# Pooled attention feeding a mixture of experts: values pooled in their own pair, slot inverse built in the first pair, last mixing in the score banks, expert 2's gathers issued earlier, three double banks for the first layer

## The chip, the cores and the metric

The kernel runs on one core of a Trainium2 chip. The metric is the device time of one execution in microseconds (us). "Clock" is the share of full speed that the throttle granted to TensorE (PE). The other engines are VectorE (DVE), ScalarE (ACT) and GpSimd (POOL); POOL also issues most DMA. A time "in the trace" counts from the span's start; an execution takes about 1.8 us more than its span. A bank is a piece of PSUM, the memory that PE's matmuls write here; DVE or ACT must copy a result out (evacuate it) before its bank is written again. Mixing is the product of attention weights and values. The slot inverse is the table that tells, for each slot of an expert, which row of x it takes. A gather fetches rows of x by index, a scatter writes output rows by index, both by DMA.

## The reference, cut to what matters

```python
# q, k, v: (8, 8, 576, 64).  Keys and values are pooled by 8 along the sequence.
k_p = k.reshape(B, H, 72, 8, D).mean(axis=3);  v_p = v.reshape(B, H, 72, 8, D).mean(axis=3)
attn = softmax(q @ k_p.T / sqrt(D));  x = attn @ v_p          # then (4608, 512): one row per token
for e in range(8):                                            # routing by a given domain_id
    out[domain_id == e] = relu(x[domain_id == e] @ w1[e]) @ w2[e]     # 512 -> 1024 -> 512
```

## The kernel before: the parts that matter

Four pairs of batches pass through attention; 16 score units and 9 mixing units a pair. Each expert has 640 slots, in five blocks of 128. The program is one list per engine, in order, made from a plan of fractional time slots (16 a pair). An instruction that has to wait holds up all that stands behind it on its engine.

```python
def big():   return ps.tile([128, 2, 512], F32, tag="big",   bufs=2)   # 2 double banks: scores, layer one
def wide():  return ps.tile([128, 8, 128], F32, tag="wide",  bufs=1)   # 1 double bank: mixing, transposes
def small(): return ps.tile([128, 512],    F32, tag="small", bufs=2)   # 2 single banks: all else
...
def av_unit(pr, cc):                                  # mixing of one chunk of 128 rows
    pv = wide();  # 8 heads of matmuls into pv
    # DVE: rcp <- 1/pv[..., 64];  x_sb <- pv * rcp;  after each third chunk x_lin <- x_sb by DMA
...
def gather(e, j, rows=XROWS): ...                     # POOL: xg[e % 2][:, j] <- rows of x_lin by index
def turn_units(e, j0, j1):                            # PE transposes xg into "wide", DVE copies to xT
def l1_units(e, ...): p = big();   ...                # 8 units: matmuls, then ReLU by ACT or DVE in turn
def l2_units(e, ...): p = small(); ...                # 1 unit per block: matmuls, copy, scatter to out
...
# the plan (slots): vp_units pool v, kp_units pool k, qt_units transpose q, all ONE PAIR AHEAD
put(kp_units(pr + 1), t0 + k0, t0 + k1); put(vp_units(pr + 1), t0 + k1, t0 + k2); put(qt_units(pr + 1), t0 + k2, t0 + k3)
put([perm_prep], 17.3, 17.3)                          # slot inverse: one set of DVE compares per pair,
for i in range(NP):                                   # then 9 matmuls; sets stand in pairs 1 and 2
    put(perm_units(i), 18.0 + 8 * i, 25.0 + 8 * i); put([perm_mm(i)], 26.5 + 8 * i, 26.5 + 8 * i)
put([perm_finish], 52.0, 52.0); put([orig_finish], 58.0, 58.0); put([count], 61.0, 61.0)
for h in range(12): put([dummy], 48.4 + h, 48.4 + h)  # 12 idle matmuls in pair 3
put([gather(0, j, XE) for j in range(3)], 57.0, 60.0); put([gather(1, j, XE) for j in range(3)], 60.0, 63.0)
put(wload_units(1, 0, 1) + wload_units(1, 1, 1), 63.1, 63.2)          # both weights of expert 1
...
run(l2_units(0, EARLY, CAP, h0))                      # experts 0 and 1 end like this:
for j in range(NBL): gather(2, j)
run(wload_units(3, 0, 1)); run(l2_units(1, EARLY, CAP, h1)); run(wload_units(3, 1, 1))
run(turn_units(2, 0, NBL))
for e in range(2, E): ...                             # l1(e) with gathers of e+1, l2(e) with transposes of e+1
```

The softmax here doesn't subtract the row's maximum and nothing guards it: scores larger than these inputs give would overflow.

## Time and profile before

| reading | value | view |
|---|---|---|
| timed runs | median 277.59 us (276.91 to 278.04) | times |
| span of the first trace | 279.4 us (that execution took 281.21) | page |
| loads | DMA share 1.0 from 10 us on | stage windows |
| first scores of pairs 0 to 3 | 20.4, 42.7, 63.8, 85.9 us | timeline of PE |
| expert 0 starts, expert 2 starts | 106.1, 156.7 us | timeline of PE |

The page shows the span in 40 equal slices; each digit is a busy share in tenths, PEclk the clock in tenths.

```profile
PE   0878878888998659988895799999989999989991
...
PEclk9999999796899956999999599999999999999997
DMA  6999999999997148937973899989979979912022
```

PE is nearly full after the middle; DMA is full until slice 12. The clock falls to 5 in two places. The stage windows give, for each stretch in us, its length, busy us and instructions of PE, PEld, DVE, ACT and POOL, then clock, DMA share and GB/s:

```profile
core 0: us, PE busy (x) PEld busy (x) DVE busy (x) ACT busy (x) POOL busy (x), PEclk, DMA share, GB/s
...
20.00:40.00 20.00, 16.41 (x258) 12.21 (x258) 6.92 (x21) 13.58 (x26) 2.11 (x4) 1.00 1.03 216
...
140.00:160.00 20.00, 14.74 (x81) 7.80 (x80) 4.46 (x8) 2.54 (x6) 11.71 (x12) 0.83 0.63 151
...
200.00:240.00 40.00, 38.37 (x256) 23.05 (x254) 13.55 (x20) 9.12 (x14) 23.87 (x26) 1.00 0.93 195
```

In 20:40 the DVE works 6.92 of 20 us. In 140:160 PE works only 14.74 of 20 us, at clock 0.83. The timelines show why. Columns: start, duration, engine, line, operation, out<-in, shape, count, and in brackets the idle time before with what ended it. First PE, then POOL:

```profile
142.26 7.07 PE L597 MATMUL small<-w,hT 128*128 128x512 f16 x32
151.06 0.40 PE L560 MATMUL turn<-ident,xg 128*128 128x128 f16 x4 [1.73 <-DMA xg<-x_lin,xrow]
...
154.96 0.61 PE L560 MATMUL turn<-ident,xg 128*128 128x128 f16 x4 [0.77 <-DMA xg<-x_lin,xrow]
156.35 0.59 PE L560 MATMUL turn<-ident,xg 128*128 128x128 f16 x4 [0.78 <-DVE xT L561]
```

```profile
146.79 0.98 POOL L606 DMA_INDIRECT out_dram<-y,tok  x1 [0.65 <-ACT y L604]
148.08 1.05 POOL L546 DMA_INDIRECT xg<-x_lin,xrow  x1 [0.30 <-issue]
```

From 149.3 to 156.4 PE does single transposes, each behind its own gather. The gathers start only at 148.08, because they stand on POOL behind the last scatter of expert 0's second layer (146.79). The view by source line puts this much idling before the mixing down to its evacuation (us, times):

```profile
  DVE x_sb L489: 12.4, 18
```

This row adds two engines that overlap: 4.8 us of PE and 7.6 us of its weight loads (PEld), as the page's groups and the view of `x_sb` show. So PE itself idled 4.8 us there.

Lastly, the dense part had pauses of 0.2 to 1.4 us in experts 2 to 6; this is one of the long ones:

```profile
206.07 1.25 PE L581 MATMUL big<-xT,v 128*128 128x320 f16 x8 [1.34 <-issue]
```

### The profile page before, as it was taken

Reading aid. Unit: us, or ns where it says so; the run is one execution under the profiler, and the core shown is the slowest. Engines: PE = TensorE matmul, PEld = TensorE weight load, DVE = VectorE, ACT = ScalarE, POOL = GpSimd, SP = SyncE. Lnnn points to the kernel's source line nnn. Section 1 sums busy time; section 2 is a strip of 40 time slices with the busy share of each in tenths; the row PEclk is TensorE's granted clock in tenths of the full one; section 3 lists DMA queues with packets and bytes.
Section 4 is the critical chain, followed back from the end, with each engine's and each line's share of the span. In section 5 each row is a group of like instructions: output and inputs, shape, how many; then the busy total and the mean of one; then the engine's idle time right before and its main releaser. Section 6 shows DMA issues by size and latency. Waiting matters only on the chain.

```text
span 279.4 us, 5003 instructions
## 1 busy us (share of the span) xinstructions
PE 236.5 (85%) x2060; PEld 148.4 (53%) x2060; DVE 125.0 (45%) x284; ACT 93.0 (33%) x157; POOL 101.1 (36%) x116
## 2 busy tenths in 40 slices
PE   0878878888998659988895799999989999989991
PEld 0666565664674336545552465655645655645640
DVE  7351449687878754432321134333333333243420
ACT  1048475484586623322220130221221311211310
POOL 7001002000000072048417864565646655724042
PEclk9999999796899956999999599999999999999997
DMA  6999999999997148937973899989979979912022
GB/s 111 216 221 212 213 219 237 239 237 245 239 229 181 60 140 161 226 91 135 241 181 123 159 221 263 169 226 189 244 164 174 235 150 196 258 61 114 20 76 106
DMA packets 18153, 50.19 MB, mean 180 GB/s; under 512 B 2316, under 2 KB 10574, under 8 KB 15568
## 3 DMA queue, kind: packets, MB, share of 16 engines
q0 software_dynamic: 16320, 45.10, 75.0%
q1 hardware_dynamic: 1808, 4.76, 4.7%
q8 instruction: 16, 0.26, 0.3%
q14 instruction: 9, 0.07, 0.1%
HBM read 67.15 MB, written 15.20 MB: 295 GB/s over the span
## 4 chain that ended last, share of the span: by engine, by line
PE 44%; issue 18%; DMA 14%; DVE 12%; POOL 8%; ACT 2%; POOLq 1%; DVEq 0%
PE big L581 17%; PE small L597 11%; DMA k<-in_k_dram 10%; POOL out_dram L606 6%; DVE x_sb L489 3%; PE wide L483 3%; PE turn L560 3%; DMA x_lin<-x_sb 3%; PE small L392 2%; PE small L421 2%; POOL xg L546 2%; PE big L463 2%; PE small L185 2%; PE small L449 1%; DMA xg<-x_lin,xrow 1%
## 5 line engine op out<-in xcount | busy, mean ns | idle before, releaser
L546 POOL DMA_INDIRECT xg<-x_lin,xrow x40 | 40.5, 1013 | 81.1 <-DVE rcp L487 53.4
L606 POOL DMA_INDIRECT out_dram<-y,tok x40 | 40.0, 1000 | 58.2 <-DVE y L602 28.4
L466 ACT ACTIVATE at<-big 72x576 f16<-72x576 f32 x64 | 40.3, 644 | 32.9 <-PE big L463 32.7
L587 DVE TENSOR_SCALAR hT<-big 128x640 f16<-128x640 f32 (+1 forms) x32 | 23.2, 725 | 53.7 <-PE big L581 45.7
L581 PE MATMUL big<-xT,w 128*128 128x320 f16 (+2 forms) x256 | 39.9, 305 | 4.0 <-issue 2.2
L597 PEld LDWEIGHTS <-hT 128*128 128x128 f16 x272 | 25.8, 98 | 28.4 <-DVE hT L587 0.7
L585 ACT ACTIVATE hT<-big 128x640 f16<-128x640 f32 (+1 forms) x32 | 19.9, 623 | 60.1 <-PE big L581 46.5
L581 PEld LDWEIGHTS <-w 128*128 128x128 f16 x256 | 24.7, 99 | 16.9 <-issue 6.0
L604 ACT ACTIVATE y<-small 128x512 f32<-128x512 f32 x20 | 11.9, 597 | 60.3 <-PE small L597 51.0
L602 DVE COPY y<-small 128x512 f32<-128x512 f32 x20 | 13.8, 691 | 31.0 <-PE small L597 27.9
L597 PE MATMUL small<-w,hT 128*128 128x512 f16 x112 | 25.8, 379 | 0.2 <-ACT hT L585 0.2
L489 DVE TENSOR_TENSOR x_sb<-wide,rcp 128x512 f16<-128x512 f32 x36 | 24.9, 691 | 1.2
L561 DVE COPY xT<-turn 128x1024 f16<-128x1024 f16 (+1 forms) x24 | 14.4, 598 | 19.6 <-PE turn L560 18.4
L483 PE MATMUL wide<-vp,at 72*128 72x65 f16 (+1 forms) x320 | 17.5, 205 | 5.4 <-DVE x_sb L489 4.8
L463 PE MATMUL big<-qT,kpT 64*72 64x288 f16 x128 | 20.5, 323 | 1.5 <-DVE qT L453 1.5
L560 PE MATMUL turn<-ident,xg 128*128 128x128 f16 x160 | 14.5, 232 | 7.0 <-DMA xg<-x_lin,xrow 4.2
L581 PE MATMUL big<-xT,k 128*128 128x320 f16 x128 | 19.7, 314 | 0.7 <-DVE hT L587 0.5
L483 PEld LDWEIGHTS <-at 72*128 72x128 f16 (+1 forms) x320 | 13.9, 107 | 11.2 <-DVE x_sb L489 7.6
L560 PEld LDWEIGHTS <-xg 128*128 128x128 f16 x160 | 11.5, 103 | 13.0 <-DMA xg<-x_lin,xrow 6.1
L597 PE MATMUL small<-v,hT 128*128 128x512 f16 x80 | 18.1, 379 | 0.0
L581 PEld LDWEIGHTS <-k 128*128 128x128 f16 x128 | 13.1, 102 | 7.1 <-issue 1.2
L421 PE MATMUL small<-ident,v 128*128 128x128 f16 x144 | 12.1, 230 | 3.1 <-DVE kpT L385 2.0
(142 smaller groups left out, 255.9 us busy)
## 6 DMA issues: line engine op xcount, KB each, us to landing
w<-in_moe_w_dram POOLq DMA_DIRECT2D x8, 1024.0 KB
k<-in_k_dram POOLq DMA_DIRECT2D x4, 1152.0 KB
q<-in_q_dram POOLq DMA_DIRECT2D x4, 1152.0 KB
v<-in_v_dram POOLq DMA_DIRECT2D x4, 1152.0 KB
x_lin<-x_sb SPq DMA_DIRECT2D x12, 384.0 KB, 7.2
k<-in_moe_w_dram POOLq DMA_DIRECT2D x3, 1024.0 KB
v<-in_moe_w_dram POOLq DMA_DIRECT2D x3, 1024.0 KB
q<-in_moe_w_dram POOLq DMA_DIRECT2D x2, 1024.0 KB
```

Of the source, the lines that this page charges most:

```text
L421: nc.tensor.matmul(pv[:, i, :], vv[:, o:o + 128], ident[:], start=(t == 0), stop=(t == 3), skip_group_check=True)
L463: nc.tensor.matmul(p[0:72, par, 0:288], s["kpT"][64 * par:64 * par + 64, bh, :], s["qT"][64 * par:64 * par + 64, :, 8 * bh:8 * bh + 8], st ...
L466: nc.scalar.activation(at[0:72, bh % 8, :].rearrange("p (a c) -> p a c", a=2), p[0:72, :, 0:288], AFT.Exp, scale=1.0 / 64.0)
L483: nc.tensor.matmul(pv[r0:r0 + z - a, h, 0:65], s["at", bt][0:72, h, a:z], s["vp"][0:72, 8 * bt + h, :], start=True, stop=True, skip_group_ ...
L489: nc.vector.tensor_tensor(out=x_sb.rearrange("p (b h a) -> p b h a", b=4, h=H), in0=pv[:, :, 0:64].rearrange("p h (a b) -> p b h a", b=4), ...
L546: i = nc.gpsimd.indirect_dma_start(out=xg[e % 2][:, j, :], out_offset=None, in_=x_lin[0:rows, :], in_offset=bass.IndirectOffsetOnAxis(ap=x ...
L560: nc.tensor.transpose(p[:, j - a, kk, :], xg[e % 2][:, j, 128 * kk:128 * kk + 128], ident[:])
L581: nc.tensor.matmul(p[:, a, 0:m], w1[:, kk, 128 * fi:128 * fi + 128], xT[:, kk, s0 + m * a:s0 + m * a + m], start=(kk == 0), stop=(kk == 3))
L585: nc.scalar.activation(dst, p[:, 0:nh, 0:m], AFT.Relu)
L587: nc.vector.tensor_scalar(out=dst, in0=p[:, 0:nh, 0:m], scalar1=0.0, scalar2=None, op0=ALU.max)
L597: nc.tensor.matmul(p[:], hT[:, fi, 128 * j:128 * j + 128], w2[:, fi, :], start=(fi == 0), stop=(fi == 7))
L606: i = nc.gpsimd.indirect_dma_start(out=out, out_offset=bass.IndirectOffsetOnAxis(ap=orig[0][:, bl:bl + 1], axis=0), in_=y[:], in_offset=No ...
```

## The change

Six things: (1) v is pooled in its own pair, after that pair's scores began; q is loaded before v, and loads are requested earlier. (2) Three of four slot-inverse sets go into pair 0, the finish into pair 2; the dummies go. (3) The last five mixings use the score banks in rotation and are packed after the scores. (4) Expert 1's first weights are requested with expert 0's. (5) Expert 2's gathers are merged into the late units of experts 0 and 1, its transposes between second-layer units. (6) Layer one rotates over three double banks, layer two over three; transposes go to "big".

```diff
+    turns = {"pre": ("big", "big", "wide"), "out": ("small", "small", "wide")}
+    def rot(kind): ...      # next tag in turn; rot2() for layer one, rot1() for layer two
-        vt[1] = load_pair(v, 1, "v")
         qt_[1] = load_pair(q, 1, "q")
+        vt[1] = load_pair(v, 1, "v")
...
-            pv = wide()
+            pv = wide() if pr < NP - 1 or cc < 4 else rot2().rearrange(...)
...
-                p = ps.tile([128, 4, 4, 128], F16, tag="wide", bufs=1, name="turn")
+                p = ps.tile([128, 2, 4, 128], F16, tag=tag, bufs=2, name="turn")   # tag: "big", early "small"
-                p = big()        # layer one
+                p = rot2()
-                p = small()      # layer two
+                p = rot1()
...
+            k0, k1 = (2.6, 6.6) if pr < NP - 1 else (3.6, 8.4)
+            put(vp_units(pr), t0 + k0, t0 + k1)
+            put(kp_units(pr + 1), t0 + 7.5, t0 + 11.0); put(qt_units(pr + 1), t0 + 11.6, t0 + 15.2)
+            # mixing slots: pair 3 gets [9.2, 10.7, 12.2, 13.7, 16.1, 16.8, 17.5, 18.2, 18.9]
...
+        put([perm_prep], 1.5, 1.5)
+        for i, (k0, k1) in enumerate(((2.0, 3.8), (4.0, 5.8), (6.0, 8.0), (18.0, 25.0))): ...
+        put([perm_finish], 40.0, 40.0); put([orig_finish], 43.0, 43.0); put([count], 46.0, 46.0)
-        for h in range(12): put([dummy], 48.4 + h, 48.4 + h)
+        put(wload_units(0, 0, 1) + wload_units(0, 1, 1), 24.0, 25.0); put(wload_units(1, 0, 1), 26.0, 26.0)
+        put(wload_units(1, 1, 1), 61.1, 61.1)               # after the early gathers, now at 55 to 61
...
-        run(merge(u, l2_units(1, 0, EARLY, he)))
+        run(merge(merge(u, l2_units(1, 0, EARLY, he)), [gather(2, j) for j in range(NBL)]))
...
+        u = l2_units(0, EARLY, CAP, h0) + l2_units(1, EARLY, CAP, h1);  t = turn_units(2, 0, NBL)
+        run([u[0], wload_units(3, 0, 1)[0], t[0], u[1], t[1], u[2], wload_units(3, 1, 1)[0], t[2], u[3]])
```

More of the change, by code (lines that the diff above doesn't have):

```diff
@@ L69, in wide, with rot, rot2, rot1 @@
         return ps.tile([128, 8, 128], F32, tag="wide", bufs=1, name="wide")
+    turns = {"pre": ("big", "big", "wide"), "out": ("small", "small", "wide")}
+    count_ = {"pre": 0, "out": 0}
+    def rot(kind):
+        i = count_[kind]
+        count_[kind] = i + 1
+        tag = turns[kind][i % 3]
+        return {"big": big, "wide": wide, "small": small}[tag]()
+    def rot2():
+        t = rot("pre")
+        ap = t[:]
+        return ap if ap.shape[2] == 512 else ap.rearrange("p (a b) c -> p a (b c)", a=2)
+    def rot1():
+        t = rot("out")
+        ap = t[:]
+        return ap if len(ap.shape) == 2 else ap.rearrange("p a b -> p (a b)")[:, 0:512]
     def small():
@@ L109 @@
         kt[1] = load_pair(k, 1, "k")
+        qt_[1] = load_pair(q, 1, "q")
         vt[1] = load_pair(v, 1, "v")
-        qt_[1] = load_pair(q, 1, "q")
         iota_f = rt.tile([128, 128], F32, name="iota_f")
@@ L473, in av_unit @@
             x_sb = s["x"][:, cc % 3, :]
-            pv = wide()
+            pv = wide() if pr < NP - 1 or cc < 4 else rot2().rearrange("p a (b c) -> p (a b) c", c=128)
             lo, hi = 128 * cc, 128 * cc + 128
@@ L499, in av_unit @@
                 tc.declare_no_dep(i.ins, group="xg", reason="the rows gathered so far are of other pairs")
-        def dummy():
-            p = small()
-            nc.tensor.matmul(p[:], ident[:], kt[NP - 1][:].rearrange("p t d -> p (t d)")[:, 0:512],
-                             start=True, stop=True)
         def merge(a, b, start=0.0):
@@ L550, in gather, with turn_units @@
             tc.add_to_no_dep_group("xg", i.ins)
-        def turn_units(e, j0, j1):
+        def turn_units(e, j0, j1, tag="big"):
             def unit(a):
@@ L594, in unit @@
             def unit(j):
-                p = small()
+                p = rot1()
                 for fi in range(8):
-                    nc.tensor.matmul(p[:], hT[:, fi, 128 * j:128 * j + 128], w2[:, fi, :],
+                    nc.tensor.matmul(p, hT[:, fi, 128 * j:128 * j + 128], w2[:, fi, :],
                                      start=(fi == 0), stop=(fi == 7))
@@ L601, in unit @@
                 if flip[0]:
-                    nc.vector.tensor_copy(y[:], p[:])
+                    nc.vector.tensor_copy(y[:], p)
                 else:
-                    nc.scalar.activation(y[:], p[:], AFT.Copy)
+                    nc.scalar.activation(y[:], p, AFT.Copy)
                 bl = NBL * e + s0 // 128 + j
@@ L637 @@
                 plan.append((t0 + h, -1, lambda pr=pr, h=h: sc_unit(pr, h)))
+            if pr + 1 < NP:
+                at = [8.6 + 1.78 * j for j in range(NC_)]
+                if pr == NP - 2:
+                    at[4:] = [16.1, 17.4, 18.8, 20.2, 21.6]
+            else:
+                at = [9.2, 10.7, 12.2, 13.7, 16.1, 16.8, 17.5, 18.2, 18.9]
             for j in range(NC_):
-                plan.append((t0 + 8.6 + j * 16.0 / 9.0, len(plan), lambda pr=pr, j=j: av_unit(pr, j)))
+                plan.append((t0 + at[j], len(plan), lambda pr=pr, j=j: av_unit(pr, j)))
+            k0, k1 = (2.6, 6.6) if pr < NP - 1 else (3.6, 8.4)
+            put([lambda pr=pr, i=i: run(vp_units_(pr, i)) for i in range(11)], t0 + k0, t0 + k1)
             if pr + 1 < NP:
-                k0, k1, k2, k3 = (7.0, 10.0, 13.6, 15.7) if pr == 0 else (2.5, 6.5, 11.6, 14.8)
-                put([lambda pr=pr, i=i: run(kp_units_(pr + 1, i)) for i in range(6)], t0 + k0, t0 + k1)
-                put([lambda pr=pr, i=i: run(vp_units_(pr + 1, i)) for i in range(11)], t0 + k1, t0 + k2)
-                put([lambda pr=pr, i=i: run(qt_units_(pr + 1, i)) for i in range(5)], t0 + k2, t0 + k3)
+                put([lambda pr=pr, i=i: run(kp_units_(pr + 1, i)) for i in range(6)], t0 + 7.5, t0 + 11.0)
+                put([lambda pr=pr, i=i: run(qt_units_(pr + 1, i)) for i in range(5)], t0 + 11.6, t0 + 15.2)
         made = {}
@@ L654 @@
         put([ovf_mm, slot_post], 0.2, 1.0)
-        put([lambda i=i: run(vp_units_(0, i)) for i in range(11)], 2.6, 6.6)
-        put([perm_prep], 17.3, 17.3)
-        for i in range(NP):
-            put(perm_units(i), 18.0 + 8 * i, 25.0 + 8 * i)
-            put([lambda i=i: perm_mm(i)], 26.5 + 8 * i, 26.5 + 8 * i)
-        put([perm_finish], 52.0, 52.0)
-        put([orig_finish], 58.0, 58.0)
-        put([count], 61.0, 61.0)
-        for h in range(12):
-            put([dummy], 48.4 + h, 48.4 + h)
+        put([perm_prep], 1.5, 1.5)
+        for i, (k0, k1) in enumerate(((2.0, 3.8), (4.0, 5.8), (6.0, 8.0), (18.0, 25.0))):
+            put(perm_units(i), k0, k1)
+            put([lambda i=i: perm_mm(i)], k1 + 0.7, k1 + 0.7)
+        put([perm_finish], 40.0, 40.0)
+        put([orig_finish], 43.0, 43.0)
+        put([count], 46.0, 46.0)
         for pr in range(2, NP):
-            for d, t_ap, tag, kx in ((kt, k, "k", 5.0), (vt, v, "v", 9.0), (qt_, q, "q", 13.0)):
+            for d, t_ap, tag, kx in ((kt, k, "k", -5.0), (qt_, q, "q", -0.6), (vt, v, "v", 7.0)):
                 put([lambda d=d, t_ap=t_ap, pr=pr, tag=tag: load(d, t_ap, pr, tag)],
-                    16 * pr - 32 + kx, 16 * pr - 32 + kx)
-        put(wload_units(0, 0, 1), 30.0, 30.0)
-        put(wload_units(0, 1, 1), 33.0, 33.0)
-        put([lambda j=j: gather(0, j, XE) for j in range(3)], 57.0, 60.0)
-        put([lambda j=j: gather(1, j, XE) for j in range(3)], 60.0, 63.0)
-        put(wload_units(1, 0, 1) + wload_units(1, 1, 1), 63.1, 63.2)
+                    max(0.1 + 0.1 * len(tag), 16 * pr - 32 + kx), max(0.1, 16 * pr - 32 + kx))
+        put(wload_units(0, 0, 1) + wload_units(0, 1, 1), 24.0, 25.0)
+        put(wload_units(1, 0, 1), 26.0, 26.0)
+        put([lambda j=j: gather(0, j, XE) for j in range(3)], 55.0, 58.0)
+        put([lambda j=j: gather(1, j, XE) for j in range(3)], 58.0, 61.0)
+        put(wload_units(1, 1, 1), 61.1, 61.1)
         put([lambda i=i: run(turn_units_(0, i)) for i in range(2)], 62.0, 64.0)
         def turn_units_(e, i):
-            return [turn_units(e, 0, 3)[i]]
+            return [turn_units(e, 0, 3, "small")[i]]
         e0 = {}
@@ L702 @@
         u = l1_units(0, EARLY, CAP, h0, 0)
-        run(merge(u, l2_units(1, 0, EARLY, he)))
+        run(merge(merge(u, l2_units(1, 0, EARLY, he)), [lambda j=j: gather(2, j) for j in range(NBL)]))
         run(turn_units(1, 3, NBL))
@@ L706 @@
         run(l1_units(1, EARLY, CAP, h1, 0))
-        run(l2_units(0, EARLY, CAP, h0))
-        for j in range(NBL):
-            gather(2, j)
-        run(wload_units(3, 0, 1))
-        run(l2_units(1, EARLY, CAP, h1))
-        run(wload_units(3, 1, 1))
-        run(turn_units(2, 0, NBL))
+        u = l2_units(0, EARLY, CAP, h0) + l2_units(1, EARLY, CAP, h1)
+        t = turn_units(2, 0, NBL)
+        run([u[0], wload_units(3, 0, 1)[0], t[0], u[1], t[1], u[2], wload_units(3, 1, 1)[0], t[2], u[3]])
         for e in range(2, E):
```

## The prediction

> # Prediction
>
> **What bounds the kernel now** differs by stage.
>
> - 0 to 45 us: loads. DMA share is 1.0 from 10 us on (stage windows); loads land about 5.5 us apart. Scores start at 20.4; the PE waits for the second pair's v (32.7) and q (38.2), and the chain of waits holds 29 us of DMA for the third pair's k.
> - 43 to 104: PE and DVE coupled in order. A pair takes about 21 us, PE busy 81 to 92%, DVE 65 to 87%. 12.4 us of PE idling before the mixing are put to its DVE evacuation (view by line). Clock 0.83 and 0.73 in 50:70, 0.55 in 100:110.
> - 104 to 157: experts 0 and 1. The last mixing ends at 113, its store lands at 121.5. From 149.3 to 157.4 the PE starves: expert 2's gathers follow the outputs one by one.
> - 157 to the end: dense PE, 19.8 us an expert, then a tail.
>
> **What the change does.**
>
> 1. v is pooled in its own pair, q loads before v: pair 1 needs q at about 32.7 instead of 38.2, and pair 0 loses 3 us of PE work.
> 2. Three of four slot-inverse sets (each about 3 us DVE, 0.5 us PE) go to pair 0, where the DVE is 20 to 50% busy. I estimate pair 0 ending near 40 us instead of 42.7, pairs 1 and 2 at 18.5 to 19 us instead of 21, so pair 3 starting near 78 instead of 86.
> 3. Twelve dummy matmuls (2.6 us of stream) leave pair 3, v pooling (3 us) enters; finishing work on the DVE goes earlier, four mixings to after the scores. I estimate 14 to 16 us of scores instead of 18, with about 2 us of wait for early gathers, whose store lands late because expert weights fill the queue until about 87.
> 4. The last five mixings use the score banks: the last x store leaves near 98 instead of 114.
> 5. Expert 2's gathers go out during expert 0's late first layer, and its transposes alternate with second-layer units: the 8.1 us gap shrinks to 1 to 2 us. Gain 6 to 7, on the critical path.
> 6. Third double bank for layer one: 1.09 us of matmuls per unit nearly hides 0.70 to 0.82 us of evacuation already. The 1.3 us pauses in most late experts are "issue", not bank waits, and stay. Gain 0 to 2.
>
> **Sum.** Score end moves from 104 to about 93 (11 us), store wait and low clock give 2 to 3, the gap 6 to 7; the dense 122 us stay. Span about 260; the timed median sits 1.8 below the span now: **259 us**, range 251 to 267. Faster 0.95, within 2% 0.04, slower 0.01.
>
> **What would show it.** Second pair's scores before 41 us, fourth's before 80; DVE fuller in 20:40; shorter mixing waits on the DVE; last x store before 101; first expert-2 first-layer matmul at 134 to 142, with no run of single transposes before it; from there about 122 us, within 2.
>
> **What would make it wrong.** DMA takes 80% of the span, about 87% of a 258 us one: weights or gathers may come late. The clock: the Trainium skill, "TensorE: Matmul & The Clock Gate", Part 1, says the default state is throttled and activity releases it; here 0.55 stands beside PE idling at 98 to 104. Without dummies pair 3 could run slow, costing 3 us or more. Pair 0 could be held by the DVE chain or the two small banks, early gathers by stores in a full queue. If pairs 1 and 2 still take 21 us, the time is about 265.

## The result, and the profile after

The changed kernel takes 265.2 us (264.77 to 265.73, 4 runs) against 277.25 us (276.09 to 278.04, 4 runs). The ratio is 0.9569, interval 0.9528 to 0.9611. A ratio is the mean time of one kernel's fast runs over the mean of the other's of the same rounds, so not quite the ratio of the medians quoted. On the chip of the last batches it was 0.9662 (0.96 to 0.9723): 265.54 against 275.06 us.

Both kernels were traced a second time there. Stage lengths in us; a pair runs from its first score unit to the next pair's, pair 3 to expert 0's first matmul. Where the prediction gives no stage length, the last column is worked out from its numbers:

| stage | before, 1st trace | before, 2nd | after, 1st | after, 2nd | predicted after |
|---|---|---|---|---|---|
| to the first scores | 20.4 | 20.1 | 20.5 | 20.6 | unchanged |
| pair 0 | 22.3 | 22.7 | 22.4 | 22.4 | 19.6 |
| pair 1 | 21.2 | 20.6 | 17.4 | 17.4 | 18.5 to 19 |
| pair 2 | 22.1 | 19.4 | 20.3 | 20.3 | 18.5 to 19 |
| pair 3 | 20.2 | 22.5 | 23.1 | 22.9 | 16 to 18 |
| experts 0 and 1 | 50.7 | 50.6 | 44.3 | 44.4 | about 42 |
| expert 2 to the end | 122.7 | 117.9 | 115.7 | 115.5 | 122 |
| span | 279.4 | 273.7 | 263.7 | 263.5 | 260 |

The two traces of the changed kernel agree within 0.2 us in every stage. Those of the kernel before do not: the first came from an execution slower than its timed runs (281.21 against 276.91 to 278.04). The second pair of traces is the fair one: 10.2 us less, of which 1.6 before expert 0, 6.2 in experts 0 and 1, and 2.4 from expert 2 on.

Its lines that answer those of before, page first, then stage windows:

```profile
PE   1785998998966867998889999999999999999990
...
PEclk9999599999995775799999999999999999999999
DMA  6999999999999934955994999989979969922022
```

```profile
20.00:40.00 20.00, 17.01 (x222) 11.51 (x222) 15.56 (x44) 10.82 (x19) 1.58 (x3) 0.83 1.04 218
...
74.00:80.00 6.00, 2.96 (x35) 2.04 (x33) 5.37 (x23) 2.67 (x4) 0.00 (x0) 0.87 1.03 244
80.00:90.00 10.00, 8.09 (x91) 5.62 (x92) 4.77 (x12) 4.99 (x9) 0.00 (x0) 0.56 1.16 245
140.00:160.00 20.00, 20.00 (x134) 12.01 (x133) 7.42 (x11) 4.17 (x7) 11.84 (x13) 1.00 0.89 191
...
200.00:240.00 40.00, 40.00 (x267) 24.07 (x266) 14.55 (x22) 9.21 (x14) 23.80 (x25) 1.00 0.81 189
```

DVE in 20:40 more than doubled, to 15.56 us, as meant. PE fills 140:160. But in 74:80 PE works 2.96 of 6 us while DVE works 5.37, and in 80:90 the clock is 0.56. The gap before expert 2 is gone; PE, then POOL:

```profile
141.74 0.61 PE L576 MATMUL turn<-ident,xg 128*128 128x128 f16 x8
142.19 1.89 PE L613 MATMUL small<-w,hT 128*128 128x512 f16 x8
...
146.31 1.89 PE L613 MATMUL small<-w,hT 128*128 128x512 f16 x8
148.03 1.25 PE L597 MATMUL big<-xT,k 128*128 128x320 f16 x8
```

```profile
127.65 1.06 POOL L562 DMA_INDIRECT xg<-x_lin,xrow  x1 [0.30 <-issue]
129.87 1.03 POOL L622 DMA_INDIRECT out_dram<-y,tok  x1 [1.17 <-ACT hT L601]
131.20 1.02 POOL L562 DMA_INDIRECT xg<-x_lin,xrow  x1 [0.30 <-issue]
```

The transposes are 0.6 us pieces between second-layer units, and the first gather stands at 127.65 instead of 148.08. The idling before the mixing did not shrink (PE 5.0 us and PEld 7.4 us of this row; in the second trace of the kernel before they were only 2.4 and 5.0):

```profile
  DVE x_sb L510: 12.4, 19
```

The chain of waits (start, us, what) and the PE timeline show what ends pair 3:

```profile
90.33 5.10 DMA x_lin<-x_sb
...
97.83 3.54 DMA xg<-x_lin,xrow
```

```profile
99.54 0.61 PE L576 MATMUL turn<-ident,xg 128*128 128x128 f16 x4 [0.96 <-DMA xg<-x_lin,xrow]
101.41 0.61 PE L576 MATMUL turn<-ident,xg 128*128 128x128 f16 x4 [1.26 <-DMA xg<-x_lin,xrow]
```

The last score unit (101.95) stands behind these two transposes, and the transposes wait for gathers, which wait for the store of pair 2's last rows.

### The profile page after: what moved, and what is told of

Same layout as the page of the kernel before. It is cut to its first block, busy times and chain, and to the rows that moved or that the text cites. A ratio compares the mean times of both kernels' runs of the same rounds, so it can differ in the third digit from the quotient of the medians.

```text
span 263.7 us, 4980 instructions
## 1 busy us (share of the span) xinstructions
PE 230.8 (88%) x2048; PEld 148.1 (56%) x2048; DVE 124.4 (47%) x284; ACT 93.4 (35%) x157; POOL 101.3 (38%) x116
## 4 chain that ended last, share of the span: by engine, by line
PE 56%; DVE 14%; DMA 10%; issue 10%; POOL 4%; ACT 3%; POOLq 1%; DVEq 0%
PE big L597 13%; PE small L613 10%; PE wide L597 6%; PE wide L613 5%; DMA x_lin<-x_sb 4%; DMA out_dram<-y,tok 4%; POOL out_dram L622 4%; PE big L484 4%; DVE x_sb L510 3%; PE wide L504 3%; PE small L442 3%; PE small L413 3%; PE small L470 2%; DMA xg<-x_lin,xrow 2%; PE turn L576 2%
## 5 line engine op out<-in xcount | busy, mean ns | idle before, releaser
L622 POOL DMA_INDIRECT out_dram<-y,tok x40 | 40.1, 1003 | 44.4 <-ACT y L620 20.7
L597 PEld LDWEIGHTS <-w 128*128 128x128 f16 x256 | 25.1, 100 | 13.9 <-issue 2.3
L603 DVE TENSOR_SCALAR hT<-big 128x640 f16<-128x640 f32 (+1 forms) x22 | 15.7, 716 | 33.1 <-PE big L597 33.1
L597 PE MATMUL big<-xT,w 128*128 128x320 f16 (+2 forms) x176 | 29.4, 312 | 1.8 <-DMA xg<-x_lin,xrow 0.9
L620 ACT ACTIVATE y<-small 128x512 f32<-128x512 f32 x14 | 8.4, 597 | 45.0 <-PE small L613 42.1
L601 ACT ACTIVATE hT<-big 128x640 f16<-128x640 f32 (+1 forms) x21 | 13.2, 627 | 29.0 <-PE big L597 29.0
L510 DVE TENSOR_TENSOR x_sb<-wide,rcp 128x512 f16<-128x512 f32 x33 | 22.8, 692 | 1.1
L484 PE MATMUL big<-qT,kpT 64*72 64x288 f16 x128 | 21.3, 338 | 2.0 <-DVE qT L474 1.9
L613 PE MATMUL small<-w,hT 128*128 128x512 f16 x80 | 18.7, 379 | 0.0
L618 DVE COPY y<-small 128x512 f32<-128x512 f32 x13 | 9.0, 692 | 20.5 <-PE small L613 19.6
L508 DVE RECIPROCAL rcp<-wide 128x8 f32<-128x8 f32 x33 | 6.8, 205 | 16.3 <-PE wide L504 16.1
L597 PE MATMUL wide<-xT,w 128*128 128x320 f16 (+2 forms) x80 | 13.3, 299 | 0.8 <-DVE xT L577 0.8
L603 DVE TENSOR_SCALAR hT<-wide 128x640 f16<-128x640 f32 (+1 forms) x10 | 7.5, 745 | 13.3 <-PE wide L597 10.1
```

Source lines behind the costliest of these rows:

```text
L484: nc.tensor.matmul(p[0:72, par, 0:288], s["kpT"][64 * par:64 * par + 64, bh, :], s["qT"][64 * par:64 * par + 64, :, 8 * bh:8 * bh + 8], st ...
L510: nc.vector.tensor_tensor(out=x_sb.rearrange("p (b h a) -> p b h a", b=4, h=H), in0=pv[:, :, 0:64].rearrange("p h (a b) -> p b h a", b=4), ...
L597: nc.tensor.matmul(p[:, a, 0:m], w1[:, kk, 128 * fi:128 * fi + 128], xT[:, kk, s0 + m * a:s0 + m * a + m], start=(kk == 0), stop=(kk == 3))
L601: nc.scalar.activation(dst, p[:, 0:nh, 0:m], AFT.Relu)
L603: nc.vector.tensor_scalar(out=dst, in0=p[:, 0:nh, 0:m], scalar1=0.0, scalar2=None, op0=ALU.max)
L613: nc.tensor.matmul(p, hT[:, fi, 128 * j:128 * j + 128], w2[:, fi, :], start=(fi == 0), stop=(fi == 7))
```

## The experiments

Ratios are against the kernel before in the same rounds. The first four ran on one chip, the other eight on another; a ratio is compared best within its chip.

### b_banks3: the banks alone

```diff
# kernel before, late experts only
-                p = big()                  # layer one; small() in layer two; transposes in "wide"
+                p = rot2()                 # rot1() in layer two; transposes in "big"
```

> The kernel before with only the three double banks for both layers of the experts (late part), transposes in the score banks. Theory A (the third bank removes the pauses of about 1.4 us in experts 2 to 6): from expert 2's first layer to the end about 116 us instead of 122.7, no second-half pause in the first layer, time about 270 to 271. Rival B (the pauses are not of the banks: instruction supply, or the timing of the gathers and loads): still about 122 us, pauses stay, time 276 to 278.

279.32 us, ratio 1.0132 (1.0068 to 1.0196): slower by about 1.3%, clear of the noise though within 2%, and above both forecasts. Expert 2 to the end took 122.3 us. No first layer paused inside any more, but PE stood still for 0.7 to 0.9 us at four changes from one layer to the other, as here:

```profile
202.83 1.25 PE L602 MATMUL wide<-xT,v 128*128 128x320 f16 x8
205.00 1.89 PE L618 MATMUL wide<-q,hT 128*128 128x512 f16 x8 [0.92 <-DVE hT L608]
```

Theory A, that a third bank brings the end down to 116 us, falls. The trace shows why: both rotations use `wide`, and where the turns of the two layers fall on it one after the other, PE waits for its evacuation (0.78, 0.92, 0.73 and 0.92 us, about 3.4 in all). In the changed kernel the two turns never meet in this way, and PE waits for nothing there. Against the 117.9 us of the kernel before in its second trace (below), 122.3 is 4.4 more, and these waits are most of it.

### a_banks2: the banks undone

```diff
# changed kernel
-                p = rot2()                 # layer one, except expert 0's early part
+                p = big()                  # small() in layer two, late transposes in "wide"
```

> The changed kernel with two banks for each layer and the transposes in the wide bank, as before; only expert 0's early layer keeps the rotation. Theory A: from expert 2 to the end 121 to 123 us with the pauses back, time about 271 to 273. Rival B: 115 to 116 us, time 265 to 266.

267.22 us, 0.9686 (0.964 to 0.9732). Expert 2 to the end: 115.8 us with two banks, 115.7 with three, and no pauses. So the banks give nothing there. They help where units are short, in expert 1. Its two first-layer parts, with two banks:

```profile
120.96 5.84 PE L597 MATMUL big<-xT,w 128*128 128x384 f16 x32 [0.89 <-DVE xT L577]
...
138.32 4.39 PE L597 MATMUL big<-xT,w 128*128 128x256 f16 x32 [0.79 <-DVE xT L577]
```

Up to the next instruction group these parts last 5.7 and 4.2 us; with three banks, at 119.6 and 136.5 us of the first trace after, 5.2 and 3.5. That is 1.2 us in all. Expert 2 started 2.5 us later than in the changed kernel; 1.1 us of this arose in expert 0's early part, which rotates in both kernels, while the clock was still low (0.56 in 110:112 against 1.00). So the run's time overstates the banks.

### a_permlate: the slot inverse where it was

```diff
-        put([perm_prep], 1.5, 1.5)         # sets 0 to 2 in pair 0, finish at 40, 43, 46
+        put([perm_prep], 17.3, 17.3)       # sets at 18 + 8 i, finish at 52, 58, 61
```

> The changed kernel with the slot inverse at the places it had before (pairs 1 and 2, finish in pair 3). Theory C (in pair 0 it costs what it saves later): pair 0 ends 2.5 to 3.5 us earlier (near 40), pair 1 and 2 take 19 to 21 us each instead of 17.4 and 20.3, and the sum is within 2 us of the changed kernel, 264 to 267. Rival D (moving it is what made pairs 1 and 2 shorter, at no cost): pair 0 stays at 42 to 43 and the time is 269 to 272.

265.46 us, 0.9636 (0.9585 to 0.9686). Pair 0 ended at 37.9 us instead of 42.9, so theory C holds for pair 0, with a cost larger than it forecast (5.0 us); pairs 1 and 2 took 20.0 and 21.3 us. The last score unit started at 101.8 us, as in the changed kernel (102.0). So moving the slot inverse into pair 0 was worth nothing here, where the early gathers held the score end (a_w1late below). The changed kernel itself did not run on this chip. What it cost there shows in the PE timeline of the changed kernel and in its stage windows (second trace):

```profile
26.39 0.50 PE L364 MATMUL small<-vc,op 128*128 128x80 f16 x9 [1.98 <-DVE vc L352]
```

```profile
24.00:26.00 2.00, 0.50 (x6) 0.23 (x4) 1.97 (x6) 1.09 (x2) 0.00 (x0) 1.00 1.06 221
...
28.00:30.00 2.00, 1.96 (x23) 1.44 (x22) 1.86 (x5) 1.87 (x5) 0.53 (x1) 0.50 1.05 221
```

PE waits 1.98 us for the DVE to finish the first set, does 0.50 us of work in 24:26, and then runs at clock 0.50. That the idling caused the low clock is likely from this order of events, not shown.

### a_vprev: v pooled a pair ahead, loads k, v, q

```diff
-            put(vp_units(pr), t0 + k0, t0 + k1)          # own pair
+            put(vp_units(pr + 1), t0 + k1, t0 + k2)      # one pair ahead; loads and their order as before
```

> The changed kernel with v pooled one pair ahead and loads in the order k, v, q, as before. Theory E (v in its own pair moves 3 us of PE work out of pair 0 and into pair 3, where it hurts): pair 3 from 23 down to about 18 to 19 us, pair 0 longer by 3 to 5 us, time within 2 us of 265. Rival F (it is a gain because q comes earlier): pair 3 stays at 22 to 23, pair 0 up by 4 to 6, time 269 or more.

268.82 us, 0.977 (0.9714 to 0.9826). Pairs 0 to 2 took 25.1, 21.4 and 20.6 us (sum 67.0 instead of 60.2), pair 3 19.8 instead of 23.1. Both theories were half right: v does burden pair 3, by 3.3 us, but it relieves the others by 6.9. On this chip the changed kernel itself did not run; the nearest neighbours, a_permlate and a_banks2, stood at 0.9636 and 0.9686. So part 1 gives about 0.8 to 1.3% (2.3 to 3.7 us); the interval is clear of the first and just overlaps the second. The edit also puts back the slots of k and q and the times of the first weight requests, so what v alone gives was not separated.

### a_gatherlate: expert 2's gathers where they were

```diff
-        run(merge(merge(u, l2_units(1, 0, EARLY, he)), [gather(2, j) for j in range(NBL)]))
+        run(merge(u, l2_units(1, 0, EARLY, he)))   # gathers after l2(0), transposes after l2(1)
```

> The changed kernel with expert 2's gathers after expert 0's second layer and its transposes at the end, as before. Theory: the gap of about 8 us before expert 2's first layer comes back, that layer starts at 153 to 155 instead of 148, time 270 to 272. If the pauses of before in experts 2 to 6 come from when gathers and weights are issued, expert 2 to the end takes 118 to 122 us besides (time 273 to 278); if they do not, it stays 115 to 116.

273.29 us, 0.9942 (0.9892 to 0.9991). The gap came back:

```profile
149.13 0.40 PE L576 MATMUL turn<-ident,xg 128*128 128x128 f16 x4 [1.61 <-DMA xg<-x_lin,xrow]
```

Expert 2 started at 154.6 us instead of 148.0, and from there to the end it took 117.2 instead of 115.7 us, with clock 0.57 in 150:156 and 0.79 in 156:160. So this one part, gathers and transposes together, is worth 273.29 minus 265.54, 7.8 us of a gain of about 10. It does not bring back pauses of the dense part.

### a_dummy: the dummies put back

```diff
+        for h in range(12): put([dummy], 48.4 + h, 48.4 + h)   # changed kernel
```

> The changed kernel with the twelve dummy matmuls of before in pair 3. Theory G (pair 3 runs at half clock because the PE idles; filling it keeps the clock): clock in 80:90 above 0.56, pair 3 shorter by 2 us or more. Rival H (pair 3 is held by the queue: the gathers land at 99 to 101 whatever the PE does): last scores again at 101.5 to 102.5 and the time 265 to 266. For the end: if the pauses of the kernel before in experts 2 to 6 come from where its PE instructions fall (24 more than in the changed kernel), they come back here and expert 2 to the end takes 118 to 122 us instead of 115.7; if not, 115 to 116.

264.76 us, 0.9636 (0.9591 to 0.968), not separated from the changed kernel on that chip (0.9662). Pair 3 began at 79.9, the last score unit stood at 101.8 and the first gather at 96.4, all as rival H forecast. But theory G was not put to the test, because the dummies did not keep the clock up:

```profile
80.00:94.00 14.00, 13.84 (x108) 8.14 (x108) 4.57 (x11) 6.19 (x11) 0.00 (x0) 0.50 1.08 242
```

The clock had fallen to 0.50 in 78:80, before the first dummy (81.1), and stayed there until 94 although PE was busy 13.84 of 14 us; in the changed kernel, without dummies, it was back at 1.00 in 90:92. With PE slow, the first transposes came at 101.0 and hardly waited for gathers (0.3 us).

Expert 2 to the end took 115.4 us, so the place of the PE instructions does not bring the pauses back either.

### a_w1late: expert 1's first weights after the early gathers

```diff
-        put(wload_units(1, 0, 1), 26.0, 26.0)
-        put(wload_units(1, 1, 1), 61.1, 61.1)
+        put(wload_units(1, 0, 1) + wload_units(1, 1, 1), 61.1, 61.2)
```

> The changed kernel with expert 1's first weights requested after the early gathers, beside its second weights, as before. Theory I (that request fills the queue before the gathers): pair 2's last store lands 2 to 3 us after issue instead of 5.1, first gather near 93 to 94 instead of 96.4, last scores at 98 to 100 instead of 102; time 262 to 264 if nothing is given back. Rival H2 (the same bytes then hold up the last x store at 110 to 116): the early gain is given back, late gathers start at 118 or later, time 265 to 267.

262.5 us, 0.9557 (0.9498 to 0.9616). The first gather started at 93.6 instead of 96.4 us, and the transposes no longer waited:

```profile
98.48 1.03 PE L576 MATMUL turn<-ident,xg 128*128 128x128 f16 x8
```

The last score unit started at 99.5 instead of 102.0, expert 0 at 101.2 instead of 103.7. Theory I holds, and nothing was given back (expert 2 at 144.2 instead of 148.0). The intervals just overlap (0.9616 against 0.96), but the traces show the mechanism. The view of `x_lin` gives the landing of pair 2's last store, issued at 90.3 in both, in the changed kernel and then here:

```profile
DMA to landing us min/median/max: 5.1/5.1/5.1
```

```profile
DMA to landing us min/median/max: 2.3/2.3/2.3
```

It landed 2.8 us sooner, and the first gather started 2.8 us sooner. The gathers themselves did not land faster (median 2.8 us from issue before, 3.4 here), so the gain is in the store's landing.

### b_nodummy: the kernel before without dummies

```diff
-        for h in range(12): put([dummy], 48.4 + h, 48.4 + h)
```

> The kernel before without its dummy matmuls. If pauses in experts 2 to 6 come from where the PE instructions fall, they vanish or move and the end takes 115 to 118 us instead of 122.7; if not, 119 to 123 us. Otherwise: if the dummies kept the clock up in pair 3, its scores end 1 to 3 us later than 103.5; if they only filled time, the same or 1 us earlier. Time 271 to 274 in the first case, 276 to 279 in the second.

274.85 us, 1.0009 (0.9955 to 1.0062): the same. The last score unit started at 100.6, with the dummies at 102.5 (before_again), so there they did not help the scores. Expert 2 to the end took 118.0 us. Taken alone this looked as if the dummies had caused the pauses; the next run says otherwise.

### before_again and after_again: second traces

```diff
# no edit
```

> The kernel before, unchanged, for a second trace. The first trace (span 279.4 us) came from an execution that took 281.2, while its timed runs took 276 to 278 and on other chips 274 to 277. If the pauses in experts 2 to 6 (5.6 us in the first trace) are of that one execution and not of the kernel, they are absent or fewer here and expert 2 to the end takes 117 to 119 us; if they are of the kernel, about 122.7 again.

> The changed kernel, unchanged, on the same chip as the two below. Same stages as in its first trace within 1 us (third pair ends at 80.6, last scores at 102, expert 2 at 148), ratio to before 0.955 to 0.963.

Before: 275.61 us, 1.0032 (0.998 to 1.0083), expert 2 to the end 117.9 us, with one wait of 0.25 us at its start and no other pause. The stage windows of this trace have

```profile
200.00:240.00 40.00, 40.00 (x272) 24.74 (x270) 14.45 (x21) 9.63 (x15) 25.70 (x27) 1.00 0.95 214
```

against 38.37 us of PE in the first trace. From expert 2 to its last matmul PE stood still 4.0 us in the first trace and 0.25 in this one (the expectation's 5.6 us is not borne out by the views). So the pauses belonged to that one execution. After: 265.54 us, 0.9662 (just above the range expected), with every stage as in its first trace.

### c_w1fin: weights late, finish of the slot inverse behind the v pooling

```diff
# a_w1late, and
-        put([orig_finish], 43.0, 43.0); put([count], 46.0, 46.0)
+        put([orig_finish], 55.5, 55.5); put([count], 56.2, 56.2)
```

> The changed kernel with expert 1's first weights after the early gathers, and the finish of the slot inverse (token numbers, overflow count) moved from the end of pair 2 into pair 3, behind the v pooling, where the DVE idles. If that DVE work held up q of pair 3 and the idling cost the PE its clock: pair 3 starts at 77 to 78.5 instead of 80.6, the stretch at 0.50 to 0.56 in 80:90 shrinks, last scores at 96 to 98.5, time 2 to 5 us below the changed kernel. If pair 3 is held by the v pooling and the mixing banks alone: starts earlier but last scores again near 99.7, no better than with the weights alone.

261.51 us, 0.9521 (0.9469 to 0.9573): faster than the changed kernel, but not separated from a_w1late (0.9557). Pair 3 started at 77.3 instead of 80.6, the last score unit at 97.9 (99.5 in a_w1late). The half clock did not go with it (0.59 in 80:90, 0.50 in 90:100), so the idling that was removed is not shown to have caused it. In the changed kernel the DVE work of the finish held PE up like this:

```profile
78.01 0.16 PE L269 MATMUL small<-nov,ones 128*128 128x2 f16 x1 [1.13 <-DVE nov L267]
...
80.62 0.46 PE L484 MATMUL big<-qT,kpT 64*72 64x288 f16 x2 [1.13 <-DVE qT L474]
```

### c_w1findum: the same with dummies

```diff
# c_w1fin, and
+        for h in range(12): put([dummy], 48.4 + h, 48.4 + h)
```

> The same with the twelve dummy matmuls of before in pair 3. If a low clock in pair 3 still costs time: 1 to 2 us faster than without them. If not: the same or 1 us slower.

260.45 us, 0.9457 (0.9413 to 0.9502). This beats both kernels: 1.9% below the changed one on the same chip, intervals apart. Stage windows of c_w1fin, then of c_w1findum:

```profile
80.00:90.00 10.00, 8.69 (x88) 6.38 (x89) 4.98 (x20) 5.64 (x11) 0.00 (x0) 0.59 1.03 245
90.00:100.00 10.00, 7.81 (x81) 4.89 (x80) 6.16 (x21) 5.17 (x9) 6.99 (x8) 0.50 0.36 111
```

```profile
80.00:90.00 10.00, 8.86 (x108) 5.30 (x107) 6.36 (x30) 7.27 (x13) 0.00 (x0) 1.00 1.04 244
90.00:100.00 10.00, 6.89 (x73) 4.10 (x70) 4.71 (x10) 3.28 (x6) 7.29 (x8) 0.68 0.38 116
```

Here the dummies kept the clock at 1.00 where it was 0.59, and in all four timed runs the mean clock was higher (0.964 to 0.973 against 0.927 to 0.942). Up to 80 us it was 1.00 in both; in a_dummy it had fallen before the first dummy. The scores ended 1.3 us earlier, but the first gathers hardly came earlier (91.2 against 91.5), and PE waited for them again (2.1 us). Expert 2 started at 143.6 against 143.0. So the 1 us between the two medians is not shown to come from the dummies; their intervals overlap.

## Why the prediction was right or wrong

The time, 265.2 us, lies in the range (251 to 267), 6 us above the middle. The direction was right, and so was the gap before expert 2, the largest gain that was measured. The largest gain forecast, 11 us at the score end, hardly came: 1.4 us by the first traces (103.8 to 102.4), 0.6 by the second. It was partly hidden by an end that was 6 us shorter than forecast, so that the time still lies in the range is in part luck. Of the prediction's own signs two held: the DVE is fuller in 20:40, and no run of single transposes stands before expert 2. The others missed: second pair's scores at 42.9 (before 41 was forecast), fourth's at 80.6 (before 80), mixing waits not shorter, last x store at 110.6 (before 101), expert 2 at 148.0 (134 to 142), and from there 115.7 us (122 within 2).

- **Step 5 (gathers of expert 2): right, slightly low.** Predicted 6 to 7 us; undoing it cost 7.8 us. The extra came after the gap, where the cold clock reached into expert 2.
- **Step 1 (v in its own pair): right, low for pair 1.** a_vprev shows 2.7 us saved in pair 0 and 3.3 us paid in pair 3, where the prediction had 3 and 3. The largest saving, 4.0 us, came in pair 1, which took 17.4 us instead of the 18.5 to 19 predicted.
- **Step 2 (slot inverse in pair 0): wrong.** It was to leave pair 0 ending near 40 us, and the text named the DVE chain as what would hold it. It ended at 42.9. The chain was worse than costed, because PE stands in order behind the first set, and its idling was followed by half clock. a_permlate shows 5 us of cost in pair 0, made up for before the score end. Pairs 1 and 2 together were right (37.7 us against 37 to 38), but pair 2 lost 3.3 us to the finish of the slot inverse (c_w1fin).
- **Step 3 (pair 3 in 14 to 16 us of scores): wrong, the largest error.** It took 21.8 us (80.6 to 102.4). What the runs show of it: v pooling costs 3.3 us, as predicted; the early gathers cost 2.2 us of waits, as predicted, and 2.5 us of score end by a_w1late. Half clock stood in 80:90; in c_w1findum the scores ended 1.3 us earlier at full clock. The base was low too: the 18 us is the first trace's, while in the second the scores of pair 3 ended 20.2 us after they began. How the rest divides between the clock and v pooling and mixing in turn on one bank pair was not separated. "Score end moves from 104 to about 93" became 102.4.
- **Step 4 (last x store near 98): failed with step 3.** It was issued at 110.6. It moved 3.6 us instead of 16.
- **Step 6 (third bank 0 to 2 us): right.** It gives about 1.2 us in expert 1's short units and nothing from expert 2 on.
- **"The dense 122 us stay": wrong in its base.** The 122.7 us held about 4 us of PE pauses of one execution; 117.9 is the kernel's figure in the other trace. It fell by 2.4 us; a_gatherlate ties about 1.5 us of that to the start of expert 2 at low clock. This made the predicted end too late and offset most of the missing 9 us at the score end.
- **The clock.** The prediction cited the Trainium skill, "TensorE: Matmul & The Clock Gate", Part 1: activity releases the throttle. The traces agree that a low clock follows idling (0.50 after PE had worked 0.50 us of 2; 0.56 in 80:90 after 2.96 us of 6). That activity releases it they show only in part: in a_dummy it stayed at 0.50 for 14 us with PE busy 13.84 of them, as the profile counts busy time. "Without dummies pair 3 could run slow" was not the whole of it: with dummies alone the clock was no better and the score end did not move; where they did keep it at 1.00 (c_w1findum), PE waited for the gathers again.

The early gathers wait for a store that shares the DMA engines with a weight load. The skill, "DMA: Bandwidth & Descriptors", Queues, rings and completion order, says that each engine serves its queues in turn, a packet at a time. This fits: the store took 5.10 us to land beside the weights and 2.3 us when the weights came later, and the gathers started 2.8 us earlier. No run here resolves single packets.

Left open: what makes the pauses of one execution; when dummies keep the clock; and what part 3 (the last mixings in the score banks) gives, since no run undoes it alone.

## What to carry to other kernels

Look for the instruction that stands in order in front of work that is ready: moving five gathers ahead of the scatters they stood behind gave most of this gain, while faster stages upstream gave none as long as transposes of late gathers stood before the last scores. Work moved into an engine's idle time is not free when another engine waits for it in order, and in these traces such waits were followed by stretches at about half clock. Idle matmuls did not bring back sooner a clock that had fallen (a_dummy), while they kept one that was still full (c_w1findum); that is one trace each. Before a stage of a trace is taken as a base, compare the traced execution's own time with the timed runs; here a difference of about 4 us was one stage's pauses. And where two rotations share a bank, look where their turns meet.

## What the Trainium skill lacked or had wrong

- "TensorE: Matmul & The Clock Gate", Why this matters for your kernels, advises to avoid PE-idle gaps over about 3 us. Here the clock halved with no gap near that: after one of 1.98 us (clock 0.50 in 28:30), and after a stretch of 6 us with PE busy 2.96 us and no gap above 1.13 us (0.56 in 80:90). The same page's "A second HAM failure mode" does speak of many small idles. What lacks is a figure for the busy share that suffices; in a_dummy 13.84 us of 14 at half clock did not.
- "Perfetto Trace Analysis", Optimizing Tensor Performance, Matmuls, says to rotate independent groups through different banks. It gives no measure of when a third bank pays: here none from expert 2 on, where a unit's matmuls last 1.09 us and an evacuation 0.70 to 0.82 us (115.8 against 115.7 us), and about 1.2 us over two parts with units of 0.44 to 0.65 us. Nor does it say what two rotations that share a bank can cost: about 3.4 us in b_banks3.
- No page that was consulted warns that one profiled execution can hold pauses that another does not have: PE stood still 4.0 us from expert 2 on in the first trace of the kernel before, 0.25 us in the second, with PE clock 1.00 in 200:240 in both.
